# Score products of a wide attention in sixteen array tiles of 32x32 instead of four of 32x128

## The chip, the cores and the metric

The kernel runs on one core of one Trainium2 chip. The metric is the device time of one launch in microseconds (us), and lower is better. A core has five engines with queues of their own: TensorE for matrix products (PE in the profile; its weight loads are shown apart as PEld), VectorE (DVE), ScalarE (ACT), GpSimd (POOL) and SyncE (SP), which here only issues DMAs. Products are written to PSUM, a memory of eight banks.

## What is computed

Two attentions over the same 2048 tokens of width 576 are mixed by a gate. Cut to what matters here:

```python
g = _sigmoid((x * gate_w).sum(-1, keepdims=True))
a = _A_ref(...)     # 64 segments of 32 tokens in turn, each with 8 memory tokens
                    # that the segment before has put out; 32 heads of width 128
b = _B_ref(...)     # softmax attention over all 2048 tokens, 32 heads of width 18
return g * a + (1 - g) * b

# in _B_ref
scores = jnp.einsum('bhqd,bhkd->bhqk', q, k) * scale
p = _softmax(scores, axis=-1)
o = jnp.einsum('bhqk,bhkd->bhqd', p, v)
```

The change is in `scores` of the second attention, which the code and this document call the wide attention: a product over only 18 elements per head, for 32 heads and 2048 x 2048 pairs of tokens.

## The kernel before

The wide attention is cut into 512 visits: 8 groups of four heads, times 4 chunks of 512 queries, times 16 blocks of 128 keys. In a visit the four heads of a group lie under one another: head j has its 18 rows of keys and queries at partitions 32j to 32j+17, and the rest of the 32 is zero. `kring` holds keys, 512 at a time (tiles `kch`), and `qring` queries (tiles `qch`), both loaded by DMA from DRAM. A visit has these steps, each an entry of the plan:

- `sb`, on TensorE (`visit`, line 932): the scores of 128 keys x 512 queries for each of the four heads. Head j takes the row strip of partitions 32j to 32j+31 of the array, and four products of 32x128 weights by 32x512 run side by side. Three results go to the three banks of the tile `sb`, the fourth to a bank `sp` of a pool of four banks that all other work shares (`pb`).
- `ex` and `ey`, on ScalarE (lines 941 and 945): the exponential of `sb` (1536 columns) and of `sp` (512 columns), written as `etb`.
- `ob`, on TensorE (`values`, line 955): four products of 128x32 weights by 128x512, in column tiles, added up over the 16 key blocks of a chunk of queries in one bank.

There is one set of `sb` banks, so the scores of a visit wait until the large exponential of the visit before has read its input, and the exponential waits for the scores.

The first attention runs between the visits, 64 segments one after another: projections in column tiles of 128x32 (`pvv`, line 1312), transposes of Q and K by DMA (`tt`), scores (`psh`, lines 1426 and 1434), sums and factors of the softmax (`pss`, line 1458; `prb`, line 1478), values (`pso`, line 1500), output projection (`acc`, line 1194) and the fold of the memory tokens into the next segment's input (`pw`, lines 1547 and 1551). `L540` is the line of a helper that copies results out of PSUM on VectorE. Matmuls without use for the result (`ob<-unit,nil`, lines 902 and 908) fill some gaps.

The order of the work on each engine is written out when the program is built. The class `Plan` is a list scheduler: each entry has engines, a duration, dependencies, a priority and a mode of the array ("row" for the scores, "col" for column tiles, "full", "tall"), and `Plan.run` places them by its own clock. It counts 0.105 us for a change of mode. It also counts the instructions of TensorE (`fetched`, with `pairs=4` for an entry unless another number is given), since those arrive in blocks. The entry of the scores is

```python
vi = add(f"sb{gq}.{kb}", "PE", 0.3, visit, [k_of[c], q_of[gq], last_vi], prio=-0.6 if gq < 2 else 0.0, mode="row", take=("sb", "pb"))
```

and its numbers are what the plan knows of it: 0.3 us, four pairs of load and matmul.

Of the kernel before, what the change touches and what calls it, by code (L numbers as in the profile page):

```python
# [110 lines left out]
class Plan:  # L111
# [59 lines left out]
    def add(  # L171
        self, name, engs, dur, fn, deps=(), prio=5.0, mode=None, take=(), give=(), tail=0.0, dmas=0, kb=0.0,
        use=None, pairs=4, alt=None, waits=0.0,
    ):
        op = Op(name, engs, dur, fn, deps, prio, mode, take, give, tail)
        op.dmas, op.kb = dmas, kb
        op.pairs, op.alt, op.form, op.waits = pairs, alt, mode, waits
        op.kind = self.kinds.setdefault(kind_of(name), len(self.kinds))
        op.use = self.ARRAY.get(mode) if use is None else use
        op.seq = len(self.ops)  # L180
        op.slots = {}
        self.ops.append(op)
        return op
# [193 lines left out]
def kernel(  # L377
# [15 lines left out]
    nc = tc.nc  # L393
    P = nc.NUM_PARTITIONS
# [77 lines left out]
    for j in range(4):  # L472
        r = slice(32 * j, 32 * j + 32)
# [52 lines left out]
    def bank(shape, dt, name, k=0):  # L526
        return ps_a.tile(shape, dt, name=name, tag=f"pb{plan.slot('pb', k)}")

    def given(pool, tag, shape, dt):
        k = plan.slot(tag)  # L530
        return pool.tile(shape, dt, name=tag, tag=f"{tag}{k}", bufs=1)
# [332 lines left out]
    def load_k(c):  # L864
        g, kc = divmod(c, NQC)
        use = visits.get(("kuse", c - NKR))


        def fn(e):
            by_head(ktd, g, slice(kc * QC, (kc + 1) * QC), kring[c % NKR], False, queue(e))  # L870

        k_of[c] = add(f"lk{c}", *carrier(4, c >= 4), fn, [use, z_k[c % NKR], *stores_for(1, g, [kc]), weight_loads["wk"][-1] if c >= 4 else None], prio=0.6, dmas=4, kb=90)

    def load_v(c):
        g, kc = divmod(c, NQC)
        use = visits.get(("vuse", c - NVR))
        hf = g // (GB // 2)

        def fn(e):
            queue(e)(  # L880
                out=vring[c % NVR][:, :].rearrange("p (k f) -> p k f", f=P),
                in_=vgd[hf][4 * kc:4 * kc + 4][:, :, g % (GB // 2), :].rearrange("k p f -> p k f"),
            )

        deps = [v_stores[hf * NKB + kb] for kb in range(4 * kc, 4 * kc + 4)]
        v_of[c] = add(f"lv{c}", *(("POOL", 0.77) if c >= 4 else carrier(1, False)), fn, [use, *deps, weight_loads["wk"][-1] if c >= 4 else None], prio=0.65, dmas=1, kb=128)

    def load_q(i):
        g, qc = divmod(i, NQC)
        use = visits.get(("quse", i - NQR))  # L890

        def fn(e):
            by_head(qtd, g, slice(qc * QC, (qc + 1) * QC), qring[i % NQR], False, queue(e))

        q_of[i] = add(f"lq{i}", *carrier(4, i >= 2), fn, [use, z_q[i % NQR], *stores_for(0, g, [qc]), weight_loads["wk"][-1] if i >= 2 else None], prio=0.55, dmas=4, kb=90)
# [19 lines left out]
    for gq in range(GB * NQC):  # L915
        RANK.update(RANKS[gq // 8])
        g, qc = divmod(gq, NQC)
        load_q(gq)
        for kb in range(NKB):
            c = 4 * g + kb // KC  # L920
            o = (kb % KC) * P
            if qc == 0 and kb % KC == 0:
                load_k(c)
                load_v(c)

            def visit(e, c=c, gq=gq, o=o, kb=kb):
                box["sb", gq, kb] = sb = ps_s.tile([P, 3, QC], FP32, name="sb")
                box["sp", gq, kb] = sp = bank([P, QC], FP32, "sp")
                kc, qt_ = kring[c % NKR], qring[gq % NQR]
                for j in range(4):  # L930
                    r = slice(32 * j, 32 * j + 32)
                    nc.tensor.matmul(  # L932
                        sb[:, j, :] if j < 3 else sp[:, :], lhsT=kc[r, o:o + P], rhs=qt_[r, :], start=True, stop=True,
                        tile_position=(32 * j, 0),
                    )

            vi = add(f"sb{gq}.{kb}", "PE", 0.3, visit, [k_of[c], q_of[gq], last_vi], prio=-0.6 if gq < 2 else 0.0, mode="row", take=("sb", "pb"))

            def expo(e, gq=gq, kb=kb):
                box["etb", gq, kb] = etb = given(bint, "etb", [P, 4, QC], BF16)  # L940
                nc.scalar.activation(out=etb[:, 0:3, :], in_=box["sb", gq, kb][:, :, :], func=ACT.Exp, scale=scale_b)  # L941

            def expo4(e, gq=gq, kb=kb):
                etb = box["etb", gq, kb]
                nc.scalar.activation(out=etb[:, 3, :], in_=box["sp", gq, kb][:, :], func=ACT.Exp, scale=scale_b)  # L945

            ex = add(f"ex{gq}.{kb}", "ACT", act_time(1536), expo, [vi], prio=0.0, take=("etb",), give=(("sb", vi, 0),))
            ey = add(f"ey{gq}.{kb}", "ACT", act_time(512), expo4, [ex], prio=0.01, give=(("pb", vi, 0),))

            def values(e, c=c, gq=gq, kb=kb, o=o):  # L950
                if kb == 0:
                    box["ob"] = ps_o.tile([P, QC], FP32, name="ob")
                ob, vc, etb = box["ob"], vring[c % NVR], box["etb", gq, kb]
                for j in range(4):
                    nc.tensor.matmul(  # L955
                        ob[32 * j:32 * j + 32, :], lhsT=vc[:, o + 32 * j:o + 32 * j + 32], rhs=etb[:, j, :],
                        start=(kb == 0), stop=(kb == NKB - 1), tile_position=(0, 32 * j), skip_group_check=True,
                    )
                if kb == NKB - 1:
                    box["ob", gq] = ob  # L960

            va = add(
                f"ob{gq}.{kb}", "PE", 0.216, values, [ex, ey, v_of[c], last_va], prio=-0.5 if gq < 2 else RANK["ob"], mode="col",
                take=("ob",) if kb == 0 else (), give=(("etb", ex, 0),),
            )
            visits[gq, kb] = (vi, ex, va)
            last_vi, last_va = vi, va
            if kb == 0:
                plan.opens.add(va)
            if kb == NKB - 1:  # L970
                plan.closes.add(va)
            if kb == 0:
                first_va = va
            if kb == NKB - 1:
                visits["quse", gq] = vi
            if qc == NQC - 1 and kb % KC == KC - 1:
                visits["kuse", c], visits["vuse", c] = vi, va

        NBK = QC // 32

        def f_turn(e, gq=gq):
            box["tq", gq] = tq = bint.tile([P, NBK, 32], FP32, name="tq")
            nc.vector.transpose(out=tq[:, :, :].rearrange("p b e -> p (b e)"), in_=box["ob", gq][:, :])

        def f_rec(e, gq=gq):
            box["rtb", gq] = rtb = bint.tile([P, NBK, 1], FP32, name="rtb")
            nc.vector.reciprocal(out=rtb[:, :, :], in_=box["tq", gq][:, :, DhB:DhB + 1])

        def f_mul(e, gq=gq):
            box["tn", gq] = tn = bint.tile([P, NBK, 32], BF16, name="tn")  # L990
            nc.vector.tensor_tensor(
                out=tn[:, :, :], in0=box["tq", gq][:, :, :],
                in1=box["rtb", gq][:, :, :].to_broadcast([P, NBK, 32]), op=ALU.mult,
            )

        def f_back(e, gq=gq):
            box["stage", gq] = stage = bint.tile([P, QC], BF16, name="stage", bufs=2)
            nc.vector.transpose(out=stage[:, :], in_=box["tn", gq][:, :, :].rearrange("p b e -> p (b e)"))  # L998

        prev = fin_state.get("back")  # L1000
        f1 = add(f"ft{gq}", "DVE", 0.7, f_turn, [va, prev], prio=0.5, give=(("ob", first_va, 0),))
        f2 = add(f"fr{gq}", "DVE", 0.26, f_rec, [f1], prio=RANK["fin"])
        f3 = add(f"fm{gq}", "DVE", 0.7, f_mul, [f2], prio=RANK["fin"])
        store2 = stages.get(gq - 2)
        f4 = add(f"fb{gq}", "DVE", 0.7, f_back, [f3, store2], prio=RANK["fin"])
        fin_state["back"] = f4
        if gq < GB * NQC - 1:
            def f_store(e, gq=gq, g=g, qc=qc):
                by_head(otd, g, slice(qc * QC, (qc + 1) * QC), box["stage", gq], True, queue(e))

            stages[gq] = add(f"fs{gq}", *carrier(4, True), f_store, [f4], prio=0.9, dmas=4, kb=90)
        else:
            stages[gq] = f4
# [696 lines left out]
    for n in range(NT):  # L1710
        qc, i = divmod(n, 4)
# [84 lines left out]
```

## Time and profile before

| | us |
|---|---|
| time, median of 3 runs | 1423.44 (1421.48 to 1425.37) |
| the profiled execution, its own time | 1421.8 |
| its span, first to last instruction | 1420.0 |
| TensorE busy | 1345.2 (95%) |
| ScalarE busy | 1091.4 (77%) |
| VectorE busy | 848.2 (60%) |
| GpSimd busy | 535.4 (38%) |

The granted TensorE clock was 0.992 of full speed over the span. In a row of groups, the parts are: line of the kernel, engine, operation, output <- inputs, shapes, number of instructions | time that the group was busy, mean duration of one in ns | idle time of the engine before them, with what ended it. In a timeline row: start, length, engine, line, operation; rows of the same kind in a row are merged (x4). "issue" means that nothing that the profile shows ended the wait. In the list of DMA queues, a row gives packets, megabytes and share of the 16 DMA engines' time; q8 brings instructions.

### The profile page before, as it was taken

Reading aid. Unit: us, or ns where it says so; the run is one execution under the profiler, and the core shown is the slowest. Engines: PE = TensorE matmul, PEld = TensorE weight load, DVE = VectorE, ACT = ScalarE, POOL = GpSimd, SP = SyncE. Lnnn points to the kernel's source line nnn. Section 1 sums busy time; section 2 is a strip of 40 time slices with the busy share of each in tenths; the row PEclk is TensorE's granted clock in tenths of the full one; section 3 lists DMA queues with packets and bytes.
Section 4 is the critical chain, followed back from the end, with each engine's and each line's share of the span. In section 5 each row is a group of like instructions: output and inputs, shape, how many; then the busy total and the mean of one; then the engine's idle time right before and its main releaser. Section 6 shows DMA issues by size and latency. Waiting matters only on the chain. (4 is left out here: it accounts for less than half of the span.)

```text
span 1420.0 us, 74484 instructions
## 1 busy us (share of the span) xinstructions
PE 1345.2 (95%) x33172; PEld 720.4 (51%) x33184; DVE 848.2 (60%) x2019; ACT 1091.4 (77%) x1277; POOL 535.4 (38%) x1162
## 2 busy tenths in 40 slices
PE   7999899999999999999999999999999999999998
PEld 4555344555554545555555544555554545444545
DVE  4443466665565566656666655656656665665566
ACT  3477688888887787887887888787778788887884
POOL 7352154334532346332543425333354324521310
PEclk9999999999999999999999999999999999999999
DMA  8787544333433344333433334333335333333335
GB/s 251 253 314 220 131 87 75 64 68 69 82 62 64 60 79 76 76 61 65 85 67 70 69 66 76 68 62 69 65 80 89 60 54 59 72 56 53 56 81 169
DMA packets 343997, 130.73 MB, mean 92 GB/s; under 512 B 296495, under 2 KB 330023, under 8 KB 343675
## 3 DMA queue, kind: packets, MB, share of 16 engines
q1 hardware_dynamic: 315155, 80.47, 29.2%
q0 software_dynamic: 26368, 43.31, 11.4%
q8 instruction: 259, 4.24, 1.3%
q10 hardware_dynamic: 2152, 2.19, 0.5%
q14 instruction: 63, 0.52, 0.1%
HBM read 52.74 MB, written 31.12 MB: 59 GB/s over the span
## 5 line engine op out<-in xcount | busy, mean ns | idle before, releaser
L941 ACT ACTIVATE etb<-sb 128x1536 bf16<-128x1536 f32 x512 | 743.5, 1452 | 227.5 <-PE sp L932 153.0
L540 DVE CAST tm<-pvv 128x512 bf16<-128x512 f32 x358 | 246.3, 688 | 230.3 <-PE pvv L1312 228.3
L945 ACT ACTIVATE etb<-sp 128x512 bf16<-128x512 f32 x512 | 305.0, 596 | 4.8 <-PE sp L932 4.8
L1312 PEld LDWEIGHTS <-ht 128*32 128x32 bf16 x7680 | 202.8, 96 | 196.2 <-issue 21.6
L932 PE MATMUL sb<-qch,kch 32*128 32x512 bf16 x1536 | 201.8, 386 | 3.2 <-ACT etb L941 1.8
L932 PE MATMUL sp<-qch,kch 32*128 32x512 bf16 x512 | 197.6, 386 | 7.6 <-DVE vl L540 5.8
L955 PE MATMUL ob<-etb,vch 128*32 128x512 bf16 x2048 | 201.9, 387 | 0.3 <-issue 0.3
L1194 PE MATMUL acc<-wo,ot 128*32 128x288 bf16 (+1 forms) x6144 | 165.7, 248 | 7.3 <-issue 3.6
L1312 PE MATMUL pvv<-wq_m,ht 128*32 128x512 bf16 x2048 | 142.1, 380 | 3.9 <-DVE ht L1559 1.5
L1312 PE MATMUL pvv<-wv_m,ht 128*32 128x512 bf16 x2048 | 141.7, 380 | 0.3 <-DVE tm L540 0.2
L1312 PE MATMUL pvv<-wk_m,ht 128*32 128x512 bf16 x2048 | 140.5, 380 | 0.1
L1194 PEld LDWEIGHTS <-ot 128*32 128x32 bf16 x6144 | 112.7, 97 | 47.0 <-DVE ot L540 17.7
L540 DVE CAST ot<-pso 128x320 bf16<-128x320 f32 x200 | 91.6, 484 | 58.3 <-PE pso L1500 57.3
L932 PEld LDWEIGHTS <-kch 32*128 32x128 bf16 x2048 | 54.5, 91 | 137.0 <-issue 121.7
L1411 DVE COPY qk<-tt 128x512 bf16<-128x512 bf16 x256 | 79.9, 314 | 54.5 <-DMA tt<-tm 51.2
L1261 POOL COPY ht<-xg 128x96 bf16<-128x96 bf16 x64 | 17.7, 277 | 236.8 <-PE pvv L1312 230.5
L955 PEld LDWEIGHTS <-vch 128*32 128x32 bf16 x2048 | 53.6, 94 | 73.5 <-issue 62.5
L851 POOL DMA_DIRECT2D qch<-qtd x120 | 61.7, 521 | 68.3 <-PE sp L932 64.6
L851 POOL DMA_DIRECT2D otd<-stage x124 | 62.8, 513 | 65.0 <-DVE stage L998 38.6
L540 DVE CAST vl<-pv 128x512 bf16<-128x512 f32 x84 | 57.2, 685 | 38.8 <-PE pv L1025 21.8
L1489 DVE TENSOR_TENSOR et<-et,prb 128x320 bf16<-128x320 bf16 x128 | 61.6, 484 | 28.0 <-PE prb L1478 23.1
L1444 ACT ACTIVATE et<-psh 128x320 bf16<-128x320 f32 x128 | 56.6, 445 | 27.0 <-PE psh L1434 25.7
(161 smaller groups left out, 1968.1 us busy)
## 6 DMA issues: line engine op xcount, KB each, us to landing
xl<-qkd SPq DMA_DIRECT2D x64, 128.0 KB
v_sb<-tm SPq DMA_DIRECT2D x256, 32.0 KB
qkd<-vl POOLq DMA_DIRECT2D x48, 128.0 KB, 2.5
wo<-in_A_Wo_dram POOLq DMA_DIRECT2D x4, 1152.0 KB, 10.9
vgd<-vt SPq DMA_DIRECT2D x32, 128.0 KB
wv_m<-in_A_Wv_dram POOLq DMA_DIRECT2D x4, 1024.0 KB
wq_m<-in_A_Wq_dram POOLq DMA_DIRECT2D x4, 1024.0 KB, 9.2
wk_m<-in_A_Wk_dram POOLq DMA_DIRECT2D x4, 1024.0 KB
```

Source lines behind the costliest of these rows:

```text
L540: nc.vector.tensor_copy(out=out_of(), in_=in_of())
L851: dma(out=rows_, in_=pads) if out else dma(out=pads, in_=rows_)
L932: nc.tensor.matmul(sb[:, j, :] if j < 3 else sp[:, :], lhsT=kc[r, o:o + P], rhs=qt_[r, :], start=True, stop=True, tile_position=(32 * j, 0),)
L941: nc.scalar.activation(out=etb[:, 0:3, :], in_=box["sb", gq, kb][:, :, :], func=ACT.Exp, scale=scale_b)
L945: nc.scalar.activation(out=etb[:, 3, :], in_=box["sp", gq, kb][:, :], func=ACT.Exp, scale=scale_b)
L955: nc.tensor.matmul(ob[32 * j:32 * j + 32, :], lhsT=vc[:, o + 32 * j:o + 32 * j + 32], rhs=etb[:, j, :], start=(kb == 0), stop=(kb == NKB - ...
L1194: nc.tensor.matmul(acc[32 * q:32 * q + 32, :], lhsT=o[:, slot, t0:t0 + CT], rhs=wo[:, h, d:d + n], start=(first and s_ == (s_ % 2 if wide ...
L1261: nc.gpsimd.tensor_copy(out=ht[:, 0:NF, M:CT], in_=xg[:, 0:NF, t])
L1312: nc.tensor.matmul(pv[32 * j:32 * j + 32, :], lhsT=ht[:, cc, :], rhs=rw, start=(c == 0), stop=(c == NF), tile_position=(0, 32 * j), skip_g ...
L1411: eng.tensor_copy(out=opened["qk"][:, hf, a, 0:16 * L].rearrange("p (j i t) -> p j i t", i=4, t=L)[:, :, :, 0:CT], in_=box["tt", s, a, hf] ...
L1444: nc.scalar.activation(out=opened["et", hf][:, :], in_=box["psh", s, hf][:, :], func=ACT.Exp, scale=scale_a)
L1489: nc.vector.tensor_tensor(out=et[:, :], in0=et[:, :], in1=box["prb", s, hf][:, :], op=ALU.mult)
```

## The change

Each head's product is cut along the keys: instead of one 32x128 tile per head, four tiles of 32x32, one per column strip of the array, each with its own weight load and its own matmul of 512 columns onto 32 partitions of the result. A visit so has 16 loads and 16 matmuls; the column strip is the outer loop, the head the inner. Banks and results stay the same. The plan's entry is the same too, with its 0.3 us and four pairs, so the plan's clock doesn't see the change and the order on all engines is the one of before.

```diff
-                for j in range(4):
-                    r = slice(32 * j, 32 * j + 32)
-                    nc.tensor.matmul(
-                        sb[:, j, :] if j < 3 else sp[:, :], lhsT=kc[r, o:o + P], rhs=qt_[r, :], start=True, stop=True,
-                        tile_position=(32 * j, 0),
-                    )
+                for i in range(0, P, 32):
+                    for j in range(4):
+                        r = slice(32 * j, 32 * j + 32)
+                        nc.tensor.matmul(
+                            sb[i:i + 32, j, :] if j < 3 else sp[i:i + 32, :], lhsT=kc[r, o + i:o + i + 32], rhs=qt_[r, :],
+                            start=True, stop=True, tile_position=(32 * j, i), skip_group_check=True,
+                        )
```

## The prediction

> **What bounds the kernel now.** I read the page first: how busy each engine is, the instruction queue, and the costliest groups.
>
> ```profile
> span 1420.0 us, 74484 instructions
> ...
> PE 1345.2 (95%) x33172; PEld 720.4 (51%) x33184; DVE 848.2 (60%) x2019; ACT 1091.4 (77%) x1277; POOL 535.4 (38%) x1162
> ...
> q8 instruction: 259, 4.24, 1.3%
> ...
> L941 ACT ACTIVATE etb<-sb 128x1536 bf16<-128x1536 f32 x512 | 743.5, 1452 | 227.5 <-PE sp L932 153.0
> ...
> L932 PE MATMUL sb<-qch,kch 32*128 32x512 bf16 x1536 | 201.8, 386 | 3.2 <-ACT etb L941 1.8
> L932 PE MATMUL sp<-qch,kch 32*128 32x512 bf16 x512 | 197.6, 386 | 7.6 <-DVE vl L540 5.8
> ```
>
> TensorE (PE) is busy 95% of the span, and ScalarE's idle time before the large exponential is mostly put down to the score products (153.0 of 227.5 us). The score rows idle 10.8 us in all over 512 visits. So TensorE's fixed order sets the pace, and what a visit gains or loses passes on. A caution: ends of matmuls are modelled (386 ns while the next group starts sooner), so I take costs from distances between starts. The next view is the timeline around one visit, with start and length in us.
>
> ```profile
> 703.07 0.39 PE L1312 MATMUL pvv<-wk_m,ht 128*32 128x512 bf16 x4
> ...
> 703.39 0.10 PEld L932 LDWEIGHTS <-kch 32*128 32x128 bf16 x4 [0.42 <-issue]
> 703.39 0.39 PE L932 MATMUL sb<-qch,kch 32*128 32x512 bf16 x3
> 703.40 0.38 PE L932 MATMUL sp<-qch,kch 32*128 32x512 bf16 x1
> ...
> 703.71 0.10 PEld L955 LDWEIGHTS <-vch 128*32 128x32 bf16 x4 [0.23 <-issue]
> ...
> 703.89 1.45 ACT L941 ACTIVATE etb<-sb 128x1536 bf16<-128x1536 f32 x1 [0.23 <-PE sp L932]
> ...
> 704.37 0.39 PE L1312 MATMUL pvv<-wk_t,ht 128*32 128x512 bf16 x4
> 704.59 0.39 PE L1312 MATMUL pvv<-wq_m,ht 128*32 128x512 bf16 x4
> ```
>
> Two groups of one shape start 0.22 us apart (704.37, 704.59): four matmuls of 512 columns run side by side. Where the shape changes, the distance is 0.32 us (703.07 to 703.39, and 703.39 to 703.71): each change of shape costs about 0.10 us. The four score matmuls start within 10 ns of each other, 3.3 ns per pair of load and matmul. Third, the waits of TensorE and one place where it waited for nothing:
>
> ```profile
> PE acc L1194 <- issue: 3.6, 2, 2.8
> ```
> ```profile
> 366.77 0.42 PE L1194 MATMUL acc<-wo,ot 128*32 128x288 bf16 x5
> 368.07 0.55 PE L1194 MATMUL acc<-wo,ot 128*32 128x288 bf16 x11 [0.88 <-issue]
> ```
>
> The second view is the timeline: in the middle of one series, with no semaphore to wait for, TensorE stands 0.88 us. I numbered the trace's TensorE records: this place and six more such stops (363.87, 387.45, 579.25, 622.16, 1291.79, 1385.91 us) all lie at record 181 to 183 of a block of 256, 1.25 to 1.5 us after a transfer of the instruction queue landed. A block of 256 is 128 pairs, 16 KB (4.24 MB over 259). These are stops for instructions, some 5 us together. The 259 instruction transfers never start closer than 3.28 us to each other, a tenth of the distances are under 3.5, the median is 4.6. A block that would be used up in less than about 3.5 us therefore stops the engine.
>
> **The change part by part.** *Removed:* 4 loads of 32x128 and 4 matmuls of 32x512 onto 128 columns, per visit. *Added:* 16 loads of 32x32 and 16 matmuls onto 32 columns each. The moving operand is read by four column strips instead of once, as line 1312's groups read four streams. Multiplications, the four PSUM banks, both changes of shape and the order on all engines stay. No DMA issue is added or moved.
>
> (1) Streaming: 16 tiles cover the array once, as four did, so 512 columns once, 213 ns (0.22 less the start). Added: 0.
>
> (2) Starts: 12 more pairs must be started before the last tile streams. Both ends of a visit are changes of shape, so the next group can't start under it, and ScalarE waits for the fifteenth matmul instead of the third. Bounds: 3.3 ns a pair, as the four above, where the pairs wait ready in TensorE's queue; 9 ns, where it has run dry, from this row (0.24 us less 167 ns of one, over 8 steps):
>
> ```profile
> 708.85 0.24 PE L1458 MATMUL pss<-bsel,et 128*32 128x2 bf16 x9
> ```
>
> 12 x 3.3 = 40 ns x 512 = 20 us; 12 x 9 = 108 ns x 512 = 55 us. Most visits come after 512-column groups that leave the sequencer time to run ahead, so I take 3.3 ns for nine tenths of them and 9 for the rest: 18 + 6 = 24 us. A rule of the Trainium skill speaks much more strongly against the change: "TensorEngine Tiling (Array Packing)", section Instruction Overhead, gives every matmul about 60 cycles (25 ns at the 2.4 GHz that the skill gives the array). That would be 12 x 25 = 300 ns a visit, 154 us. The trace has 25 ns only between matmuls of the *same* tile (the 40-column products of line 1434: 8 rounds of 4 begin some 25 ns apart); neighbours in other tiles start 3.3 ns apart. All 16 are different tiles, so I go by the row.
>
> (3) Loads: 32 columns instead of 128. The first group after a change starts its matmul 4 ns after its load in both widths, and line 955's 32-column loads take 94 ns against 91. Gain 0; at most the 10 ns by which a 512-column group after a change runs longer (0.228 against 0.217 us), 5 us.
>
> (4) Instructions: 512 x 24 = 12,288 more, 48 blocks: 259 become 307. In the single records the blocks' own distances are 3.7 us for the quickest tenth, 4.0 at a quarter, 4.6 in the middle. A block holds two visits on average; 24 more pairs shrink its old content to 128/152 = 0.84, and the longer visits add 0.07: 3.2, 3.4, 3.9 us. With a floor of 3.5 us some 27% of 307 blocks, 83, fall under it, by 0.2 us on average: 17 us, less the 5 lost now: 12 us. With a floor of 3.3 it is 52 blocks by 0.15, 8 less 5: 3 us; with 3.7, 123 by 0.28, 34 less 5: 29 us. "Runtime: NRT & Kernel Launch", section Instruction fetch mechanics, calls the crossing of a block mostly hidden: 0 us. The stops above show that it isn't at the dense places, so I take 12.
>
> (5) What hides it: TensorE waits about 1 us per segment for VectorE (lines 1434, 1478, 1547). A delay goes into such a wait only where it falls between the awaited work's own start on TensorE and the wait: for the transposed Q and K one or two visits (line 1434's 10.5 us in 24 waits), for the others hardly any. I take 4 us back, at most 10. If that cover is gone, nothing is taken back. Late next is the exponential of each visit, by 40 ns; its order on ScalarE is fixed and its next input comes equally late.
>
> Sum: 24 + 12 - 4 = 32 us. The profiled execution took 1421.8 us (span 1420.0 and 1.8 around it), 1.6 under the median of 1423.4; I add to the median: **1455 us**.
>
> **The rivals.**
> *Nearly hidden* (0.09): 3.3 ns for all, the low floor, the high cover: 20 + 3 - 10 = 13 us, 1436, and down to 1428. For it: ScalarE has 23% free. Against: the chain of a visit runs through both engines.
> *Instructions become the bound* (0.22): blocks at the floor follow one another, the queue is empty behind each, visits there start at 9 ns a pair. A third of the visits at 9 ns, which adds 0.33 x 12 x 5.7 ns x 512 = 12 us: 20 + 12 = 32 for the starts, floor 3.7: 29; 61 us, 1484; to 1505 with half of them slow. For it: 54 of 229 blocks between 250 and 1390 us already take under 4.0 us. Against: only seven stops now.
> *Tiles of one row strip don't overlap* (0.06): they share the moving data's rows; then 4 x 213 ns, 0.64 us more a visit, +327 us, 1750. Against: the 128x32 groups feed four column tiles from the same rows at once at 0.22 us. Sixteen at once no row here shows; "TensorE: Matmul & The Clock Gate", Part 3, Measured speedup vs the span model, has them in parallel.
> *Faster* (0.04): smaller tiles empty sooner. The place is the change of shape, 0.10 us on each side of a visit. If each side fell to 0.06, a visit would shed 80 ns, 41 us, against the 32 of the sum: 9 us won, 1414. It decides from 32 us / 512 = 63 ns a visit. Against: the distance after 32x128 and after 128x32 groups is the same 0.32 us, so the shape doesn't set it.
> *No difference* (0.02): the same with about 63 ns.
>
> **How the numbers follow.** The main case, 1438 to 1472, has 0.57: (2) between 20 and 35, (4) between 3 and 20. No change is what lies within 0.3% (4 us), about what a measurement of this kernel can tell. Faster 0.04, same 0.02, slower 0.94. The range leaves out the serial case, the faster ones, and the ends of the first two rivals: 1434 to 1492.
>
> **What would show it.** Right: the 16 starts spread over 50 to 60 ns, the distance from visit to next group 0.36 to 0.38 us instead of 0.327; 307 instruction transfers; more stops at record 182 of a block; ScalarE's and VectorE's durations unchanged. Wrong: a spread over 100 ns at most visits (issue set too low), 0.85 us and more from a visit to the next group (no overlap), a change of shape under 0.08 us (faster), or instruction transfers closer than 3.2 us.

## The result, and the profile after

The changed kernel takes 1478.3 us (median of 4 runs, 1475.7 to 1480.7) against 1424.4 us of before beside it: 1.0375 times as long, with a 95% interval of 1.0341 to 1.0409, or 54 us more. In a second set of six runs, made beside the later experiments, it came out at 1.0367 (1.0333 to 1.0400). The forecast was 1455 us with a range of 1434 to 1492. The direction and the range held; the increase was 54 us and not 32, and the likeliest case ended at 1472.

The page after, in the lines that answer to those shown of before (line numbers are one higher behind the change):

```profile
span 1476.0 us, 86768 instructions
...
PE 1379.9 (93%) x39312; PEld 747.2 (51%) x39328; DVE 847.8 (57%) x2019; ACT 1096.7 (74%) x1277; POOL 534.9 (36%) x1162
...
q8 instruction: 307, 5.03, 1.5%
...
L942 ACT ACTIVATE etb<-sb 128x1536 bf16<-128x1536 f32 x512 | 743.5, 1452 | 284.6 <-PE sp L933 212.7
...
L933 PE MATMUL sb<-qch,kch 32*32 32x512 bf16 x6144 | 236.4, 386 | 8.1 <-ACT etb L942 2.0
L933 PE MATMUL sp<-qch,kch 32*32 32x512 bf16 x2048 | 223.6, 386 | 10.4 <-DVE vl L540 6.4
```

ScalarE's exponentials last exactly as long as before (1452 ns), and its idle time before them grew by 57 us (284.6 against 227.5), with more of it put down to the score products (212.7 against 153.0). TensorE's busy share fell by two points although it has more to do: it stands still for longer. There are 48 more transfers of instructions, as counted.

One visit in the timeline after:

```profile
730.87 0.14 PEld L933 LDWEIGHTS <-kch 32*32 32x32 bf16 x16 [0.24 <-issue]
730.87 0.39 PE L933 MATMUL sb<-qch,kch 32*32 32x512 bf16 x3
730.88 0.38 PE L933 MATMUL sp<-qch,kch 32*32 32x512 bf16 x1
...
730.91 0.39 PE L933 MATMUL sb<-qch,kch 32*32 32x512 bf16 x3
730.92 0.39 PE L933 MATMUL sp<-qch,kch 32*32 32x512 bf16 x1
731.23 0.27 PEld L1501 LDWEIGHTS <-v_sb 64*128 64x128 bf16 x16 [0.23 <-issue]
```

All sixteen start within 50 ns, and the next group follows 0.36 us after the first start, where it was 0.32. Over all visits, the median spread of the starts went from 10 to 50 ns, and the distance to the next group from 325 to 365 ns. That is 12 pairs at 3.3 ns, to the nanosecond. The pace held everywhere: in none of the 512 visits is the median distance between two starts over 4 ns. The 58 visits that spread over more than 60 ns have a gap between one matmul and the next, 42 of them before the fourth, the first that writes the shared bank `sp`.

And one visit in which a block of instructions ended:

```profile
727.52 0.39 PE L933 MATMUL sb<-qch,kch 32*32 32x512 bf16 x3
727.57 0.37 PE L933 MATMUL sp<-qch,kch 32*32 32x512 bf16 x1
...
727.60 0.38 PE L933 MATMUL sp<-qch,kch 32*32 32x512 bf16 x1
727.92 0.39 PE L933 MATMUL sb<-qch,kch 32*32 32x512 bf16 x3
727.93 0.38 PE L933 MATMUL sp<-qch,kch 32*32 32x512 bf16 x1
```

Twelve of its matmuls start by 727.60, the last four at 727.92. No semaphore is waited for in between; 727.92 is the first record of a block of 256, and 1.26 us earlier a transfer of instructions landed. Such stops, found as in the prediction (a wide gap at the first record of a block, 1.1 to 1.65 us after a transfer landed), are 66 after and were 7 before. The counts depend on the least gap that is called wide: from 0.2 us on they are 80 and 9, from 0.3 us on 60 and 4. The list of waits shows them as "issue", spread over many lines:

```profile
PE acc L1195 <- issue: 4.1, 7, 1.0
PE pv L1030 <- issue: 3.3, 6, 1.2
...
PE sb L933 <- issue: 1.8, 5, 0.8
PE prb L1479 <- issue: 1.7, 3, 0.9
```

**Where the 56 us of span went.** Both kernels issue the same groups in the same order on TensorE, so the distance from the start of each group to the start of the next can be compared pair by pair. I put each into one of three kinds: those in which a block of instructions ends, the other visits, and everything else. After less before, in us (the second profile is that of the repeat, `e9_again`):

| profile, against before | a block ends | other visits | the rest | sum | stops |
|---|---|---|---|---|---|
| the changed kernel | +38.9 | +28.6 | -12.0 | +55.5 | 66 |
| the same, second profile | +34.4 | +26.5 | -9.2 | +51.7 | 56 |

The rows are not pure. "The rest" holds -4.9 us for stops of before, whose blocks now end elsewhere; what remains, -7 and -4, is mostly shorter waits for other engines. Where a block ends, 63 groups are visits, whose longer starts make 2.5 us of that column. And "other visits" are some 450, for which 40 ns each make 18 us; half of the remaining 10.6 is one wait, which the list of waits of after has and that of before has not:

```profile
PE pvv L1313 <- POOL ht L1262: 5.3, 1, 5.3
```

TensorE stands there at 132 us, behind a visit, for a copy on GpSimd that itself waits 6.8 us for a DMA (`xg<-xtd`) issued at the same time as in before (125.9 against 126.0 us). The second profile has the same wait (5.2 us), and so have three of the experiments below (`e1_queries` 3.2, `e3_sparse` 4.8, `e8_wide` 4.8); the others and before do not. Why the transfer lands late in some runs stays open; it is neither a longer start nor a stop for instructions.

### The profile page after: what moved, and what is told of

Its sections match the earlier page's. It is cut to its first block, busy times and chain, and to the rows that moved or that the text cites. A ratio compares the mean times of both kernels' runs of the same rounds, so it can differ in the third digit from the quotient of the medians.

```text
span 1476.0 us, 86768 instructions
## 1 busy us (share of the span) xinstructions
PE 1379.9 (93%) x39312; PEld 747.2 (51%) x39328; DVE 847.8 (57%) x2019; ACT 1096.7 (74%) x1277; POOL 534.9 (36%) x1162
## 3 DMA queue, kind: packets, MB, share of 16 engines
q0 software_dynamic: 26368, 43.31, 10.6%
## 4 chain that ended last, share of the span: by engine, by line
PE 66%; DMA 16%; DVE 10%; issue 4%; ACT 2%; SPq 1%; POOL 0%; ACTq 0%; DVEq 0%; POOLq 0%
PE pvv L1313 22%; DMA tt<-tm 10%; PE acc L1195 9%; PE sb L933 9%; PE ob L956 7%; PE pso L1501 3%; PE pv L1026 3%; DVE tm L540 2%; PE pv L1030 2%; ACT etb L942 2%; PE pq L734 2%; PE pvb L773 1%; PE prb L1479 1%; PE psh L1435 1%; DMA v_sb<-tm 1%
## 5 line engine op out<-in xcount | busy, mean ns | idle before, releaser
L942 ACT ACTIVATE etb<-sb 128x1536 bf16<-128x1536 f32 x512 | 743.5, 1452 | 284.6 <-PE sp L933 212.7
L933 PE MATMUL sb<-qch,kch 32*32 32x512 bf16 x6144 | 236.4, 386 | 8.1 <-ACT etb L942 2.0
L933 PE MATMUL sp<-qch,kch 32*32 32x512 bf16 x2048 | 223.6, 386 | 10.4 <-DVE vl L540 6.4
L933 PEld LDWEIGHTS <-kch 32*32 32x32 bf16 x8192 | 78.3, 88 | 159.9 <-issue 141.6
```

Source lines behind the costliest of these rows:

```text
L933: nc.tensor.matmul(sb[i:i + 32, j, :] if j < 3 else sp[i:i + 32, :], lhsT=kc[r, o + i:o + i + 32], rhs=qt_[r, :], start=True, stop=True, t ...
```

## The experiments

Theory A: 20 us or so come with the longer visits, and the larger part with blocks of instructions that run out. Theory B: the longer visit is all of it, by late exponentials behind it; the number of instructions costs nothing by itself. Later runs add theory C: every block of instructions costs its share, about 1 us, wherever it lies. Times are medians; a ratio is to the runs of before that were made together with them (medians 1419.6, 1421.3 and 1419.5 us), and "us more" is worked out from the ratio. Diffs are cut to the lines that matter, and that of the first run shows only the new ones; they are against the changed kernel, those of "The time alone" and "One product per filler" against before.

### The instructions alone

```diff
+                for q0 in range(0, QC, 128):
                     for j in range(4):
+                        r, qs = slice(32 * j, 32 * j + 32), slice(q0, q0 + 128)
                         nc.tensor.matmul(
+                            sb[:, j, qs] if j < 3 else sp[:, qs], lhsT=kc[r, o:o + P], rhs=qt_[r, qs],
+                            start=True, stop=True, tile_position=(32 * j, 0), skip_group_check=True,
                         )
```

> A visit again has sixteen pairs of load and matmul, in the same places of the same order, but cut along the queries: four rounds of 128 columns in the four 32x128 row tiles. So TensorE gets exactly as many instructions as in the changed kernel (307 blocks), and a visit streams 4 x 128 = 512 columns per tile as before, some 10 ns longer instead of 40. Theory A (starts of 20 us and stops for instructions of 28 us or so, side by side): 5 us for the length and 25 to 30 for the stops, 1450 to 1460 us, with 50 to 70 stops at block boundaries. Theory B (the longer visit is all of it, by late exponentials and dry queues; the number of instructions costs nothing by itself): 1424 to 1432 us.

Measured: 1466.5 us, ratio 1.0326 (1.0305 to 1.0347), 46 us more. The distance from a visit to the next group is 333 ns at the median, 8 more than before. The page and the rows of the scores:

```profile
span 1461.1 us, 86768 instructions
...
q8 instruction: 307, 5.03, 1.5%
```
```profile
L933 PEld LDWEIGHTS <-kch x8192: 90/93/147, 26.9 to 1442.4; 32*128 32x128 bf16 x200
L933 PE MATMUL sb<-qch,kch x6144: 211/214/310, 26.9 to 1442.4; 32*128 32x128 bf16 x199
```

The second is the view of one source line (lowest, median and highest ns). There are the changed kernel's 307 blocks, full 128-column tiles, and hardly a longer visit (8 ns x 512 = 4 us), and yet most of the loss: 62 stops, +35.6 us where a block ends. Theory B would have had 1432 at most. Theory A's range ended 6 us too low; 3.2 us are the late transfer of above.

### The time alone

```diff
-                for j in range(4):
+                for j, n in ((0, 96), (0, QC), (1, QC), (2, QC), (3, QC)):
                     r = slice(32 * j, 32 * j + 32)
                     nc.tensor.matmul(
-                        sb[:, j, :] if j < 3 else sp[:, :], lhsT=kc[r, o:o + P], rhs=qt_[r, :], start=True, stop=True,
-                        tile_position=(32 * j, 0),
+                        sb[:, j, 0:n] if j < 3 else sp[:, :], lhsT=kc[r, o:o + P], rhs=qt_[r, 0:n], start=True, stop=True,
+                        tile_position=(32 * j, 0), skip_group_check=True,
                     )
```

> A visit is made 40 ns longer with almost no instructions: the four 32x128 products stay, and ahead of them head 0's first 96 columns are computed once more into the same place (96 columns at 2.4 per ns are 40 ns; the results are the same). One pair more per visit, 512 in all, 4 blocks. Theory A: 20 us of length and 1 to 4 us of stops, 1443 to 1449 us, with 7 to 15 stops at block boundaries. Theory B: the 54 us of the changed kernel come with the 40 ns, 1470 to 1480 us.

Measured: 1432.2 us, ratio 1.0069 (1.0046 to 1.0092), 10 us more. The visits came out 33 ns longer (358 against 325), which alone would be 17 us. The comparison of distances gives +18.0 for the visits, +9.2 where a block ends (23 stops: even 512 pairs more bring some), and -14.4 for the rest. So theory B falls here too, and theory A's own figure for the length is too high: more than half of what the visits and the stops lose in this run is waited less elsewhere. The changed kernel against the run with the instructions alone points the same way, less firmly: 32 ns x 512 = 16 us more of visit, 8 us more of time by the ratios, but 15 and 11 by the two profiles.

### Where the instructions stand

Half of the 512 visits get sixteen tiles, chosen by the number of TensorE pairs that the plan puts within 2.5 us of the visit:

```diff
+        order = self.run()
+        pe = [op for op in order if op.eng == "PE"]
...
+        near = {}
+        for op in pe:
+            if op.name.startswith("sb"):
+                near[op.name] = sum(n_of[id(x)] for x in pe if abs(x.start - op.start) < 2.5)
+        ranked = sorted(near, key=lambda k: near[k])
+        self.split = set(ranked[:256])    # the other run: ranked[256:]
```

> Sixteen tiles only in the half of the visits with the fewest TensorE pairs near them in the plan (on average 85 pairs within 2.5 us of the visit), four tiles in the others. 24 more blocks. Theory A: 256 x 40 ns = 10 us, and few stops since these blocks last long: 2 to 6 us, 1436 to 1441 us. Theory B (every visit costs the same 0.105 us): 27 us, 1451 us.

> The other half: sixteen tiles only in the 256 visits with the most pairs near them (on average 157 within 2.5 us). 24 more blocks, as many as in the sparse half. Theory A: 10 us for the starts and 18 to 26 us of stops, 1452 to 1460 us, 40 stops or more at block boundaries. Theory B: 27 us, 1451 us, the same as the sparse half.

Measured: sparse 1443.2 us, ratio 1.0172 (1.0147 to 1.0197), 24 us more, 19 stops; dense 1460.1 us, ratio 1.0288 (1.0264 to 1.0312), 41 us more, 61 stops. Both have 283 blocks and 256 long visits, and theory B asked for equal times. The difference is where a block ends: +13.7 us in the sparse half, +39.5 in the dense one. In the list of waits of the dense half and then of the sparse half the same row reads

```profile
PE acc L1212 <- issue: 7.1, 13, 1.0
```
```profile
PE acc L1212 <- issue: 5.6, 8, 1.5
```

The sparse half was dearer than I had expected (24 us, not 16 to 21): its visits rose by 18.5 us in the profile, where 256 x 40 ns are 10. The distances show where: the visits that moved by less than 0.1 us give 8.5 us, and 25 others 10.0, of which 4.9 are the late transfer of above,

```profile
PE pvv L1330 <- POOL ht L1279: 4.8, 1, 4.8
```

and 2.0 a single visit at 26 us; the profiled execution was also 7 us above the median of its kernel. So the theory's 10 us for the starts held. The halves' extra times add up to 65 us against 54 for both together; that a stop in one place spares one elsewhere would explain it, but isn't shown.

### Eight tiles

```diff
-                for i in range(0, P, 32):
+                for i in range(0, P, 64):
...
-                            sb[i:i + 32, j, :] if j < 3 else sp[i:i + 32, :], lhsT=kc[r, o + i:o + i + 32], rhs=qt_[r, :],
+                            sb[i:i + 64, j, :] if j < 3 else sp[i:i + 64, :], lhsT=kc[r, o + i:o + i + 64], rhs=qt_[r, :],
```

> Eight tiles of 32x64 in each visit instead of sixteen of 32x32: 4 pairs more than before the change instead of 12, 275 blocks. Theory A (blocks of instructions that run out in under about 3.75 us stop TensorE; the longer visit is mostly taken up by waits): a third of the starts, 13 ns a visit or 7 us, of which half stays, and some 8 to 14 us of stops (20 to 30 of them): 10 to 18 us over before, 1430 to 1438 us on a chip where before takes 1420. Theory C (a third of the pairs costs a third): 18 us. Theory B (the cost is in tiles that are narrower than the array, whatever their width): as much as sixteen tiles, 54 us.

Measured: 1437.6 us, ratio 1.0128 (1.0098 to 1.0159), 18 us, at the edge of theory A and just what a third costs; it doesn't part A from C. (The B of this run, that narrow tiles cost by themselves, asked for 54 us and falls.) It has 25 stops and +14.7 us where a block ends. The starts spread over 23 ns, 13 more than before, as expected, but the next group comes 27 ns later. The groups by shape, of this run and of the changed kernel, hold a candidate for the other 14:

```profile
L933 PEld LDWEIGHTS <-kch 32*64 32x64 bf16 x4096 | 70.9, 101 | 146.8 <-issue 128.6 <-DMA kch<-ktd 3.4 <-DVE lbf L1220 0.5
```
```profile
L933 PEld LDWEIGHTS <-kch 32*32 32x32 bf16 x8192 | 78.3, 88 | 159.9 <-issue 141.6 <-DMA kch<-ktd 3.7 <-DVE lbf L1220 0.6
```

A load of 64 columns takes 101 ns, one of 32 takes 88, and one of 128 took 91 before. That the slower load is what holds the next group back was not tested.

### The plan told of it

```diff
-            vi = add(f"sb{gq}.{kb}", "PE", 0.3, visit, ..., mode="row", take=("sb", "pb"))
+            vi = add(f"sb{gq}.{kb}", "PE", 0.34, visit, ..., mode="row", take=("sb", "pb"), pairs=16)
```

> The sixteen tiles, and the plan is told of them: 0.34 us instead of 0.3 and 16 pairs instead of 4 per visit, so that its own count of instruction blocks sees them and it orders all work anew. Theory A: the plan moves dense work away from the places where a block would run out, so fewer stops; but it was searched for another load and fills in more idle matmuls (some 1,920 rows of fillers instead of 1,119), so the sum may go either way: 1440 to 1490 us, with fewer than 66 stops. Theory B (the visit's length is all): no gain from the count of pairs, 1474 us or more, stops as before.

Measured: 1548.7 us, ratio 1.0898 (1.0867 to 1.0929), far outside theory A's range; B's open end allows it, though not by its reasons. It has 61 stops, hardly fewer, and 960 column-tile filler matmuls instead of 552. Both numbers of the plan changed, and with them the whole order, so the run doesn't part the two theories, and what made the new order slow wasn't looked into.

### The loops the other way round

```diff
-                for i in range(0, P, 32):
-                    for j in range(4):
+                for j in range(4):
+                    for i in range(0, P, 32):
```

> The sixteen tiles with the loops the other way round: the four column strips of one head one after another, then the next head. Same instructions, same blocks. If loads and starts in one row strip hinder each other, a visit's starts spread over more than the 50 ns of the changed kernel, 100 to 160 ns, and it gets 10 to 40 us slower than the changed kernel; if only the pace of issue counts (theory A), the spread stays 50 ns and the time is the changed kernel's within 5 us: 54 us over before.

Measured: 1466.9 us, ratio 1.0325 (1.0299 to 1.0351), 46 us. The spread is 50 ns and the distance 365 ns as with the heads inside, so loads and starts in one row strip don't hinder each other. It has 59 stops. The changed kernel itself ran once more:

> The changed kernel itself once more, beside the others of this call, since the runs so far stood on several chips: 50 to 56 us over before, against 46 for the sixteen tiles with the heads outside and 46 for the products cut along the queries. Should it come out at 46 to 48, the order of the loops makes no difference.

Measured: 1472.7 us, ratio 1.0367 (1.0333 to 1.0400), 53 us. The interval overlaps that of the other loop order by a little. With the heads outside, the three heads that the large exponential reads are issued after 12 of 16 pairs instead of 15, but the profiles point elsewhere: that of the changed kernel has the wait of 5.2 us for the late transfer and that of the other order has not, and without it the two profiled executions (1472.1 and 1464.1 us of span) are 3 us apart. So no gain of the order is shown.

### Pairs taken out elsewhere

With sixteen tiles, and with the four of before; the plan keeps its old numbers and so its order:

```diff
-                wo_loads, ("pb",), [[o] for o in ots[2 * hf:2 * hf + 2]], wide=not hf,
+                wo_loads, ("pb",), [[o] for o in ots[2 * hf:2 * hf + 2]], wide=True, planned=not hf,
...
-                out=opened["obf"][:, s % 4, 0:RW], in0=st["acc"][:, :], in1=st0["sum"][:, 0:RW], op=ALU.add
+                out=opened["obf"][:, s % 4, 0:RW], in0=st["acc"][:, 0:RW], in1=st0["sum"][:, 0:RW], op=ALU.add
```

> The sixteen tiles, and pairs taken out elsewhere: the output projection of the second half of the heads (line 1194 of before) is issued as 32 products of 288 columns per segment, two side by side per head, instead of 64 of 144. TensorE streams as long as before and the plan's order is the same, but there are 2,048 pairs less, 16 blocks, all out of dense places; the partial sums of half of them are not added up, so part of the first attention's result is left out. Theory A: the stops fall from 66 to 35 or 50, 8 to 20 us faster than the changed kernel, 35 to 46 us over before. Theory B (the visits are all of it): no change, 54 us over before.

Measured: 1458.4 us, ratio 1.0271 (1.0231 to 1.0310), 39 us over before and so some 14 us less than the changed kernel (1.0375 and 1.0367). The stops fell from 66 to 27, below what I expected, for 16 blocks less. The visits are as long as in the changed kernel (365 ns). So part of the loss can be taken back at a place that the change doesn't touch, here at the price of sums that are left out.

> The kernel before with its four tiles, and with the same pairs taken out of the output projection as in the wide run with sixteen tiles (2,048 pairs, 243 blocks; the partial sums of half of the second half's heads are not added up, so part of the first attention's result is left out). Theory A (a block costs only where it runs out early, and before had seven such places, 5 us): 2 to 6 us faster than before. Theory C (each block costs its share everywhere, about 46 us / 48 blocks = 1 us, in both directions): 16 us faster.

Measured: 1417.6 us, ratio 0.9988 (0.9974 to 1.0003): no gain that can be told from none, and 6 stops instead of 7. A microsecond per block in both directions (theory C) would have been 16 us and is ruled out. A block costs where it runs out, and before it hardly did.

### One product per filler

```diff
     def warm_col(e):
-        for j in range(4):
+        for j in range(1):
```

> The kernel before with one product per filler instead of four: a filler streams as long, with a quarter of the pairs (414 pairs less, 3 blocks). Theory A: the fillers lie where TensorE waits, so the blocks around them are not the ones that run out: within 4 us of before, and boundaries that move give some chance of either sign. A granted clock under 0.98 would show that the fillers' four tiles are needed.

Measured: 1426.2 us, ratio 1.0048 (1.0029 to 1.0067), 7 us slower with three blocks *less*, and 14 stops instead of 7; the granted clock stayed at 0.992. The boundaries of the blocks had moved, and the order was laid out for where they were. That is likely but only argued: I didn't move the boundaries alone.

No version beat the kernel before beyond the uncertainty of its time.

## Why the prediction was right or wrong

The direction and the range were right; the increase was forecast at 32 us and came out at 54, beyond the main case. The range held because it left room for the rivals; one term of the sum was far too small.

**What bounds the kernel**: right as far as it goes. TensorE's order sets the pace. Its waits can take back a good deal of what is added: half in the run with the longer visits alone.

**Streaming, step (1)**: right. 365 - 325 = 40 ns is all starts, with nothing for sixteen streams: they do run side by side. A fixed overhead for each matmul would have made it 300 ns a visit. The Trainium skill, "TensorEngine Tiling (Array Packing)", section Instruction Overhead, also says that a product of 1 column takes as long as one of 60. That makes the 60 cycles a least time; added to products of 512 columns, as the prediction did for comparison, they don't fit the 40 ns of the trace.

**Starts, step (2)**: the pace of 3.3 ns was right to the nanosecond and makes 512 x 40 ns = 20.5 us, against 24 forecast. The tenth of the visits at 9 ns, 6 us of those 24, didn't come: no visit started at that pace, not even behind a stop. The 28.6 and 26.5 us of the table are higher by other waits, 5 us of them for the late transfer, which nobody forecast.

**Loads, step (3)**: right for 32 columns (88 ns, no gain). The eight tiles show that it was no general rule: 64 columns load more slowly than 128.

**Instructions, step (4)**: this is the step that failed, by its size. Forecast 12 us net of the 5 lost before. Measured, the table's 38.9 us less 2.5 for the visits in it and less those 4.9 are 31.5; the same in the second profile gives 27. With nearly nothing but the instructions changed, 35.6 us stand in that column. The stops were found rightly, but the floor was the wrong measure. I took 3.5 us, from how close the *quicker* transfers start to each other (6% of the distances, not a tenth, are under it). At a place that stops, the whole way from the first record of one block to the first of the next is 3.75 us at the median after (quartiles 3.59 and 4.00), made up of 1.2 us until the transfer starts, 1.1 for the transfer and 1.4 from its landing to the first instruction. Six of the seven stops of before already read 3.6 to 4.2 there (the seventh 6.1), so the number could have been had. My own upper end, with a floor of 3.7, was 29 us.

Yet 3.75 us is no sharp limit either. Each of the 307 blocks has its own transfer, and none started sooner than 1.2 us after that had landed; when the transfer starts varies. After the change 41 blocks passed in under 3.6 us without a stop, and their transfers had started 0.6 us at the median behind the first record of the block before, instead of 1.2.

The second fault is the even spread: I shortened all blocks by 0.84 and took 0.2 us for each that fell under the floor. The stops are fewer (66, not 83) and longer: the gap is 0.51 us at the median. They gather where other work stands close: the dense half has 61, the sparse half 19.

**The rule of the Trainium skill in step (4)**: "Runtime: NRT & Kernel Launch", section Instruction fetch mechanics, calls the crossing mostly hidden. For 241 of the 307 blocks of the changed kernel that is so; the other 66 make up most of the loss. Weighing the row above the rule was right.

**Cover, step (5)**: forecast 4 us and at most 10. The table's -12.0 and -9.2 look like more, but without the stops of before they are -7 and -4, and other waits at visits, new or longer (5 and 3 us), take most of that back: 1 to 2 us net. In the run with the longer visits alone the waits gave some 14 back, so what they cover depends on where the delay falls.

**The sum**: 24 + 12 - 4 = 32 was forecast. In the same terms 20.5 + 31.5 - 1.8 came, and 5.3 for the late transfer: 55.5 us. The rival "instructions become the bound" comes nearest with 61 us: its 29 for the stops was close, its 32 for the starts was not, since the slow visits behind empty queues, which it took for its own sign, never showed. (Its upper end of 1505 doesn't follow from its terms: with half of the visits at 9 ns they give 20 + 18 + 29 = 67 us, 1490.) The serial case, the faster one and no change are out.

## What to carry to other kernels

When a change multiplies small instructions on an engine that is nearly full, cost the instructions themselves. Find the record at which a series stops with nothing to wait for, see whether those places repeat with a fixed count, and measure the way from one block to the next where it *did* stop. That is nearer to the budget of a block than the average rate or the quickest transfers, though not a sharp limit, and the dense stretches are where it is broken. Longer visits cost about half of their length where waits followed, while the stops were hard to hide: the same twelve pairs cost 46 us with hardly a longer visit, and the longer visit without them 10.

And when distances are compared group by group, look at the few that moved most. A single late transfer was 5 us here, and it sat in a row that seemed to measure something else.

## What was not expected of the hardware

- A weight load of 64 columns takes longer (101 ns) than one of 32 (88 ns) or of 128 (91 ns), and a visit of eight 32x64 tiles is 14 ns longer than its starts explain.
- Sixteen tiles of 32x32 start 3.3 ns apart in either order of the loops, also four in a row in one row strip, and also behind a stop.
- Three blocks of instructions fewer, with moved boundaries, made the kernel 0.48% slower (0.29 to 0.67%).
